# Divisors of the first attention batch through DRAM, weight pieces on SyncE's queue, additions behind both thresholds

## The chip, the cores and the metric

The kernel runs on one core of a Trainium2 chip. The metric is device time in microseconds (us). TensorE is called PE here, its weight loads PEld, VectorE DVE, ScalarE ACT, GpSimd POOL, and SyncE SP. An instruction that starts a transfer sits in the queue of the engine that issues it: POOL's transfers form one queue (q0, software), SP's another (q1, hardware), ACT's a third (q10).

## The reference

A thresholded attention, and then a two-layer network with an exact GELU on its output. All is float32, but the two weight matrices come as float64.

```python
# q, k, v: (8 batches, 8 heads, 576 positions, 64); tau = 0.02
scores = scale * q @ k.T                      # scale = 1/sqrt(64)
thresh = max(scores, -1) - tau
scores = where(scores >= thresh, scores, -1e9)
attn = exp(scores - max(scores))
attn = attn / (sum(attn, -1) + 1e-9)
x = (attn @ v) laid out as (8*576, 512)
h = x @ w_in                                  # w_in (512, 2048), float64
g = 0.5 * h * (1 + erf(h / sqrt(2)))
out = g @ w_out                               # w_out (2048, 512), float64
```

## The kernel before, in words

**Slots.** Two heads make a pair `p`; four pairs (`HP`) make a batch, 32 pairs (`NP`) in all. The 576 positions of a pair are cut into four chunks of 128 and a tail of 64 (`NC` = 4). One turn of the main loop over `n` is a *slot*: one chunk `i` of one pair, with both heads in it (for the tail, i = 4, the two heads' 64 positions share one tile of 128 rows). The first batch (`p < EARLY`, slots 0 to 19) runs in two halves: slots 0 to 7 are chunks 0 and 1 of pairs 0, 1, 2, 3; slots 8 to 19 are chunks 2, 3, 4 of the same pairs. Later batches take a pair at a time. The order of instructions on every engine is that of the program; there is no planner.

**What a slot does.** `scores` puts q·k of one chunk into PSUM (PE, L410, two buffers, one for each head). `softmax_head` takes the negated maximum `nmx` of each head (DVE, L422), makes the threshold `thr` from it (POOL, L423) and the exponentials `p` (ACT, L425). `softmax_tail` (DVE, L442) sets to zero what is below the threshold and sums the rest into a divisor; only then are the score buffers free for the next slot's PE work. One slot later `turn_p_early` turns `p` by PE (L356) and ACT copies the result to `pT` (L363, L372). Two slots after a chunk, `weigh_v` or `weigh_half` multiply by v (L545, L569), ACT copies to `xall`, and `divide_early` divides.

**Divisors of the first batch.** POOL adds 1e-9 to each pair of sums (L445), DVE takes the reciprocal in the next slot (`invert`, L451), and `divide_early` spreads the column of 128 reciprocals over 64 rows by a matmul with an identity (PE, L464; ten instructions per pair), ACT copies this to `inv` (L466), and POOL multiplies `xall` by it (L472). It happens in slots 3, 5, 7 and 9 (chunks 0 and 1 of pairs 0 to 3) and in slots 12, 15, 18 and 21 (the rest).

**Divisors of later batches.** `divisors`: DVE adds 1e-9 to all sums of a pair (L480), takes reciprocals (L481) and transposes the tile in blocks of 32 (L483); SP writes it to DRAM (L486) and reads it back so that each row reaches 64 partitions (L492, L494).

**Weights.** The 32 weight pieces (128 x 512 float64, 512 KB each) are loaded into staging places (parts of `xall` and `turned_p`), and turned into float32 during the first batch. `load_piece` starts one load (L183): pieces 0 and 1 from ACT's queue, all others from POOL's. Four are started ahead of slot 0, four more in slots 0 and 2, and then one whenever a piece has left its place. The conversion of a piece is two ACT operations (L202, L203), two DVE operations on integers (L210, L212) and an integer addition on POOL (L226, `add_low_bits`). `convert` at the end of a slot emits some 1.8 pieces' worth; the additions that are due are emitted in the next slot: one right behind the threshold of each head, and what is left behind the second.

**SP before.** In the first batch SP issues the loads of q, k and v of pairs 1 to 3 and of v of pair 0, and then of pairs 4 and 5 (`load`), whose v loads wait for a POOL memset (L264).

**The network.** From slot 8 on `fill` puts matmuls of the first layer (L637) between the steps of the attention, and later of the second (L652); a matmul is emitted only when its weight pieces are converted in program order. `keep_busy` adds idle matmuls in three slots.

Of the kernel before, what the change touches and what calls it, by code (L numbers as in the profile page):

```python
# [8 lines left out]
FP32 = mybir.dt.float32  # L9
# [3 lines left out]
ALU = mybir.AluOpType  # L13
# [5 lines left out]
def kernel(  # L19
# [138 lines left out]
    loaded = [0]  # L158
    converted = [0]

    def load_piece(eng=nc.gpsimd):
        k = loaded[0]
        if k == len(pieces):
            return
        staged = k % 2 and k < len(pieces) - LATER
        if wide and not staged and not x_free:
            return
        dst, src = pieces[k]
        loaded[0] += 1
        if not wide:  # L170
            nc.sync.dma_start(dst, src)
            converted[0] += 1
            load_piece()
            return
        slot = []
        if staged:

            half, at = divmod(k // 2 % 4, 2)
            raw = pd[half].bitcast(U32)[:, at * 2 * PIECE:(at + 1) * 2 * PIECE]
        else:  # L180
            slot = [x_slot()]
            raw = x_rows(slot[0]).bitcast(U32)
        eng.dma_start(raw, src.bitcast(U32))  # L183
        raws.append((dst, raw, slot))
# [228 lines left out]
    def softmax_head(p, i):  # L413

        s = st[p]
        n = len(s["sc", i])
        nmx = small.tile([P, 2], FP32, tag="nmx", name="nmx")
        thr = s["thr", i] = small.tile([P, 2], FP32, tag="thr", name="thr")
        w = s["p", i] = work.tile([P, 2 * S], FP32, tag="p", name="p")
        for e in range(n):  # L420
            sc = s["sc", i][e][:, :, 0:HALF]
            nc.vector.tensor_reduce(nmx[:, e:e + 1], sc, axis=AXIS.XY, op=ALU.max, negate=True)  # L422
            nc.gpsimd.tensor_scalar(  # L423
                thr[:, e:e + 1], nmx[:, e:e + 1], -1.0, tau_eff, op0=ALU.mult, op1=ALU.subtract)
            nc.scalar.activation(  # L425
                w[:, e * S:(e + 1) * S].rearrange("p (h s) -> p h s", h=2), sc, AF.Exp, bias=nmx[:, e:e + 1], scale=1.0)
            add_low_bits(1)

    def softmax_tail(p, i):

        s = st[p]
        sc, thr, w = s.pop(("sc", i)), s.pop(("thr", i)), s["p", i]
        n = len(sc)
        if p < EARLY:
            pair = small.tile([P, 2], FP32, tag="den", name="den", bufs=2 * SLOTS)
            den = [pair[:, e:e + 1] for e in range(n)]
        else:
            at = [e * NC + i if i < NC else 2 * NC for e in range(n)]
            den = [sums[p % 2][:, x:x + 1] for x in at]
        for e in range(n):  # L440
            row = w[:, e * S:(e + 1) * S].rearrange("p (h s) -> p h s", h=2)
            nc.vector.scalar_tensor_tensor(  # L442
                row, sc[e][:, :, 0:HALF], thr[:, e:e + 1], row, op0=ALU.is_ge, op1=ALU.mult, accum_out=den[e])
        if p < EARLY:
            nc.gpsimd.tensor_scalar(pair[:, 0:n], pair[:, 0:n], 1e-9, None, op0=ALU.add)  # L445
            s["sum", i] = pair[:, 0:n]

    def invert(p, i):

        den = st[p]["sum", i]  # L450
        nc.vector.reciprocal(den, den)  # L451

    def divide_early(p, lo, hi):


        s = st[p]
        b, hp = divmod(p, HP)
        tr = ps.tile([P, 512], FP32, tag="mm", name="tr")
        for i in range(lo // P, -(-hi // P)):
            den = s.pop(("sum", i))  # L460
            to = tr[:, i * P - lo:min((i + 1) * P, hi) - lo]
            for e in range(2):
                one_of, cols = (den[:, e:e + 1], ident) if i < NC else (den, ident[:, e * TAIL:(e + 1) * TAIL])
                nc.tensor.matmul(to[e * D:(e + 1) * D, :], lhsT=one_of.to_broadcast([P, D]), rhs=cols, start=True, stop=True)  # L464
        by = dg.tile([P, S], FP32, tag="inv", name="inv")
        nc.scalar.copy(by[:, 0:hi - lo], tr[:, 0:hi - lo])  # L466
        for n, o, at, size in in_blocks(b, lo, hi):
            x, y = x_blk[n][:, hp, o:o + size], by[:, at - lo:at - lo + size]
            if size == TOK:
                x = x.rearrange("q (p c) -> q c p", c=2)  # L470
                y = y.rearrange("q (c p) -> q c p", c=2)
            nc.gpsimd.tensor_tensor(x, x, y, op=ALU.mult)  # L472

    def divisors(p):

# [10 lines left out]
        flat = rows.rearrange("a k i -> a (k i)")  # L488
        for e in range(2):
            to = t[e * D:(e + 1) * D]  # L490
            src = flat[:, e * P:(e + 1) * P].unsqueeze(0).to_broadcast([D, 4, P])
            eng.dma_start(to[:, 0:MAIN].rearrange("p (a x) -> p a x", x=P), src)  # L492
            src = rows[2 * e:2 * e + 2, 2 * NC, :].unsqueeze(0).to_broadcast([D, 2, Q])
# [597 lines left out]
    for n in range(len(slots) + WEIGH + 1):  # L1091
# [3 lines left out]
        if p < NP:  # L1095
            scores(p, i)
            softmax_head(p, i)
            add_low_bits()
            if last and last[0] < EARLY:
                invert(*last)  # L1100
            if p < HP - 1 and i == 0:
                turn_qk_early(p + 1)
        elif n == len(slots):
# [26 lines left out]
            turn_p_early(*last)  # L1130
        if p < NP:
            softmax_tail(p, i)
        if p < NP and not early:
            turn_p(p, i)
        if p < NP and not early:
# [89 lines left out]
```

## Time and profile before

| | |
|---|---|
| median of 3 runs | 1340.18 us (1338.49 to 1342.54) |
| the profiled execution | 1340.39 us, of which the span is 1338.6 |
| PE busy | 1320.5 us, 99% of the span |
| DVE / ACT / POOL busy | 1043.3 / 604.9 / 656.0 us |
| granted PE clock | 1.00 |
| first batch, slots 0 to 19 | 10 to 136 us |
| chain that ended last | PE 93%, DVE 2%, DMA, ACT, POOL and issue 1% each |

The slots can be found in the trace by the start of their maximum (L422): slot 0 at 10.16 us, 1 at 15.18, 2 at 19.70, 3 at 24.70, 4 at 31.15, 5 at 36.68, 6 at 43.12, 7 at 49.12, 8 at 54.80, 9 at 61.13, 10 at 67.20, 11 at 71.73, 12 at 77.71, 13 at 86.00, 14 at 91.25, 15 at 97.10, 16 at 106.29, 17 at 111.75, 18 at 118.75, 19 at 125.38, 20 at 130.12.

A busy PE is not a PE at its peak: the ends of matmuls are modelled, and a matmul that waits in the pipeline counts as busy. So the chain of waits and the order in time say more here than the share of busy time. The trace holds two records for each float32 matmul instruction.

### The profile page before, as it was taken

How to read it: one execution, taken by the hardware profiler on the slowest of the kernel's cores; microseconds unless marked ns; L12 is line 12 of the kernel's file. 1: busy time of each engine (PE TensorE's matmuls, PEld its weight loads, DVE VectorE, ACT ScalarE, POOL GpSimd, SP SyncE). 2: the span in 40 equal slices, each digit the busy share in tenths (PEclk: the TensorE clock that was granted, in tenths of full speed). 3: DMA queues.
4: the chain of work that ended last, by engine and by line, in shares of the span. 5: the costliest groups of instructions: out<-in, count | busy, mean ns of one | idle time of the engine just before them, and what ended most of it. 6: DMA issues, size and time to landing. Idle time of an engine off the chain costs nothing.

```text
span 1338.6 us, 19954 instructions
## 1 busy us (share of the span) xinstructions
PE 1320.5 (99%) x6354; PEld 893.9 (67%) x6354; DVE 1043.3 (78%) x2005; ACT 604.9 (45%) x1029; POOL 656.0 (49%) x1091
## 2 busy tenths in 40 slices
PE   8899999999999999999999999999999999999998
PEld 6677466466466466457557557568787787877877
DVE  6877778788888888888888888784857698385775
ACT  7877458258357358338438437322211113211120
POOL 5875455555555556545555551245264503635530
PEclk9999999999999999999999999999999999999999
DMA  8652565776786786786787776400000130000003
GB/s 266 190 164 46 121 151 137 166 185 154 173 190 153 176 204 153 176 213 155 164 216 166 162 187 128 108 9 0 1 0 1 38 99 22 1 1 0 1 0 79
DMA packets 209783, 152.41 MB, mean 114 GB/s; under 512 B 113360, under 2 KB 193088, under 8 KB 209680
## 3 DMA queue, kind: packets, MB, share of 16 engines
q1 hardware_dynamic: 187648, 110.43, 36.1%
q0 software_dynamic: 21312, 39.37, 10.7%
q10 hardware_dynamic: 720, 1.34, 0.4%
q8 instruction: 52, 0.85, 0.3%
q14 instruction: 51, 0.42, 0.1%
HBM read 55.97 MB, written 12.52 MB: 51 GB/s over the span
## 4 chain that ended last, share of the span: by engine, by line
PE 93%; DVE 2%; DMA 1%; ACT 1%; POOL 1%; issue 1%; SPq 0%; DVEq 0%; POOLq 0%; ACTq 0%
PE bank L825 34%; PE o_ps L652 17%; PE hT L637 16%; PE sc L410 13%; PE xT L545 12%; DMA q<-in_q_dram 1%; DVE power L212 1%; DMA v<-in_v_dram 1%; POOL w_in L226 1%; DVE nmx L422 0%; PE tr L356 0%; ACT p L425 0%; DVE power L210 0%; ACT pT L363 0%; PE tr L464 0%
## 5 line engine op out<-in xcount | busy, mean ns | idle before, releaser
L425 ACT ACTIVATE p<-sc,nmx 128x576 f32<-128x576 f32 x288 | 201.7, 738 | 275.0 <-DVE nmx L422 274.8
L442 DVE SCALAR_TENSOR_TENSOR p<-sc,thr,p 128x576 f32<-128x576 f32 x288 | 226.4, 816 | 78.1 <-ACT p L425 68.2
L423 POOL TENSOR_SCALAR thr<-nmx,tau_eff 128x1 f32<-128x1 f32 x288 | 84.5, 293 | 359.8 <-DVE nmx L422 350.3
L637 PE MATMUL hT<-xall,w_in 128*128 128x256 f32 x1024 | 242.0, 386 | 0.2 <-POOL xall L472 0.2
L422 DVE TENSOR_REDUCE nmx<-sc 128x1 f32<-128x576 f32 x288 | 205.4, 750 | 43.7 <-PE sc L410 42.4
L652 PE MATMUL o_ps<-w_out,g 128*128 128x512 f32 x512 | 236.8, 603 | 0.0
L637 PEld LDWEIGHTS hT<-xall,w_in 128*128 128x128 f32 x1024 | 189.3, 190 | 50.5 <-issue 23.0
L707 DVE TENSOR_TENSOR c<-c,bank 128x320 f32<-128x320 f32 x304 | 147.0, 487 | 33.8 <-PE bank L825 20.5
L707 DVE TENSOR_TENSOR o<-o,bank 128x256 f32<-128x256 f32 x240 | 99.8, 419 | 93.7 <-PE bank L825 88.7
L652 PEld LDWEIGHTS o_ps<-w_out,g 128*128 128x128 f32 x512 | 93.1, 190 | 109.1 <-issue 106.3
L410 PE MATMUL sc<-kT,qT 64*128 64x288 f32 x960 | 161.3, 429 | 2.6 <-DVE p L442 2.6
L545 PE MATMUL xT<-pT,v 128*64 128x320 f32 (+1 forms) x1240 | 159.6, 409 | 0.7 <-DVE pT L367 0.5
L506 DVE STREAM_TRANSPOSE turned_p<-p 128x1152 f32<-128x1152 f32 x112 | 154.4, 1378 | 3.9
L410 PEld LDWEIGHTS sc<-kT,qT 64*128 64x128 f32 x960 | 91.8, 186 | 77.2 <-issue 62.5
L545 PEld LDWEIGHTS xT<-pT,v 128*64 128x64 f32 x1240 | 86.5, 137 | 71.5 <-issue 10.8
L825 PE MATMUL bank<-w_out,c 128*128 128x256 f32 x480 | 120.2, 381 | 0.5 <-DVE o L707 0.5
L269 POOL DMA_DIRECT2D v<-in_v_dram x208 | 110.9, 536 | 4.1 <-issue 2.2
L825 PEld LDWEIGHTS bank<-w_out,c 128*128 128x128 f32 x480 | 89.9, 190 | 18.8 <-DVE o L707 3.0
L878 ACT ACTIVATE c<-c 128x320 f32<-128x320 f32 (+1 forms) x80 | 46.9, 624 | 114.6 <-DVE c L707 114.5
L707 POOL TENSOR_TENSOR c<-c,g 128x320 f32<-128x320 f32 (+1 forms) x40 | 50.5, 1271 | 67.5 <-DVE c L707 67.5
L825 PE MATMUL bank<-t_out,c 128*128 128x256 f32 x320 | 82.8, 381 | 0.0
L825 PE MATMUL bank<-t_out,g 128*128 128x256 f32 x320 | 82.1, 379 | 0.0
(184 smaller groups left out, 1785.5 us busy)
## 6 DMA issues: line engine op xcount, KB each, us to landing
pT<-turned_p SPq DMA_DIRECT2D x448, 160.0 KB, 3.6
pT<-pd_tail SPq DMA_DIRECT2D x112, 80.0 KB, 2.9
q<-in_q_dram POOLq DMA_DIRECT2D x104, 72.0 KB, 3.6
k<-in_k_dram POOLq DMA_DIRECT2D x104, 72.0 KB, 3.1
inv<-turned SPq DMA_DIRECT2D x54, 128.0 KB, 4.0
v<-in_v_dram POOLq DMA_DIRECT2D x156, 40.0 KB, 3.0
out_dram<-o SPq DMA_DIRECT2D x40, 128.0 KB, 2.3
xall<-in_moe_w_out_dram POOLq DMA_DIRECT2D x9, 512.0 KB, 4.2
```

The source lines that it names most:

```text
L269: eng.dma_start(t[r:P:4, e, 0:n, :], rows[:, r * KR:r * KR + n, :])
L410: nc.tensor.matmul(sc[e][:, h, 0:HALF], lhsT=lhsT, rhs=s["kT"][rows, at:at + HALF], start=True, stop=True)
L422: nc.vector.tensor_reduce(nmx[:, e:e + 1], sc, axis=AXIS.XY, op=ALU.max, negate=True)
L423: nc.gpsimd.tensor_scalar(thr[:, e:e + 1], nmx[:, e:e + 1], -1.0, tau_eff, op0=ALU.mult, op1=ALU.subtract)
L425: nc.scalar.activation(w[:, e * S:(e + 1) * S].rearrange("p (h s) -> p h s", h=2), sc, AF.Exp, bias=nmx[:, e:e + 1], scale=1.0)
L442: nc.vector.scalar_tensor_tensor(row, sc[e][:, :, 0:HALF], thr[:, e:e + 1], row, op0=ALU.is_ge, op1=ALU.mult, accum_out=den[e])
L506: nc.vector.transpose(turned_p[:, :, i // 2, 0:NB, i % 2 * Q:(i % 2 + 1) * Q], w.rearrange("p (e b i) -> p e b i", e=2, i=Q))
L545: nc.tensor.matmul(to, lhsT=s["v"][:, e, c, :], rhs=rhs, start=(c == 0), stop=(c == KR - 1))
L637: nc.tensor.matmul(hT[:, j % 2, :], lhsT=w_in_sb[c][:, j * P:(j + 1) * P], rhs=x_blk[n][:, c, :], start=(c == 0), stop=(c == N_DM - 1))
L652: nc.tensor.matmul(o[:, 0:d_model], lhsT=g[j][:, m * P:(m + 1) * P], rhs=w_out_sb[j], start=(j == 0), stop=(j == N_DF - 1))
L707: eng.tensor_tensor(out, a, b, op=ALU.add)
L825: nc.tensor.matmul(to, lhsT=l, rhs=r, start=start and k == 0, stop=k == len(pairs) - 1, skip_group_check=not start)
```

## The change

Three edits, all of which act in the first batch.

1. The divisors of the first batch go through `divisors` too. It is called at the end of `softmax_tail`'s slot for chunk 1 (for chunks 0 and 1) and for the tail (for the others), with a layout of its own for the two halves; `divide_early` keeps only POOL's multiplication, two slots later as before. L445, L451, L464 and L466 go.
2. `load_piece` issues from SP's queue unless told otherwise. Pieces 0 and 1 stay on ACT's queue, 2 and 3 on POOL's; the other 28 move from POOL to SP, each to its place in SP's program order.
3. The call of `add_low_bits(1)` inside the loop over the heads goes. All additions that are due come behind both thresholds of a slot.

```diff
-    def load_piece(eng=nc.gpsimd):
+    def load_piece(eng=nc.sync):
...
             nc.scalar.activation(
                 w[:, e * S:(e + 1) * S].rearrange("p (h s) -> p h s", h=2), sc, AF.Exp, bias=nmx[:, e:e + 1], scale=1.0)
-            add_low_bits(1)
...
-        if p < EARLY:
-            pair = small.tile([P, 2], FP32, tag="den", name="den", bufs=2 * SLOTS)
-            den = [pair[:, e:e + 1] for e in range(n)]
-        else:
-            at = [e * NC + i if i < NC else 2 * NC for e in range(n)]
-            den = [sums[p % 2][:, x:x + 1] for x in at]
+        at = [e * NC + i if i < NC else 2 * NC for e in range(n)]
+        den = [sums[p % 2][:, x:x + 1] for x in at]
...
-        if p < EARLY:
-            nc.gpsimd.tensor_scalar(pair[:, 0:n], pair[:, 0:n], 1e-9, None, op0=ALU.add)
-            s["sum", i] = pair[:, 0:n]
-
-    def invert(p, i):
-
-        den = st[p]["sum", i]
-        nc.vector.reciprocal(den, den)
-
     def divide_early(p, lo, hi):
-        s = st[p]
         b, hp = divmod(p, HP)
-        tr = ps.tile([P, 512], FP32, tag="mm", name="tr")
-        for i in range(lo // P, -(-hi // P)):
-            den = s.pop(("sum", i))
-            to = tr[:, i * P - lo:min((i + 1) * P, hi) - lo]
-            for e in range(2):
-                one_of, cols = (den[:, e:e + 1], ident) if i < NC else (den, ident[:, e * TAIL:(e + 1) * TAIL])
-                nc.tensor.matmul(to[e * D:(e + 1) * D, :], lhsT=one_of.to_broadcast([P, D]), rhs=cols, start=True, stop=True)
-        by = dg.tile([P, S], FP32, tag="inv", name="inv")
-        nc.scalar.copy(by[:, 0:hi - lo], tr[:, 0:hi - lo])
+        by = st[p].pop("inv")
         for n, o, at, size in in_blocks(b, lo, hi):
             x, y = x_blk[n][:, hp, o:o + size], by[:, at - lo:at - lo + size]
             if size == TOK:
-                x = x.rearrange("q (p c) -> q c p", c=2)
-                y = y.rearrange("q (c p) -> q c p", c=2)
+                x = x.rearrange("q (a i c) -> q a c i", i=Q, c=2)
+                y = y.rearrange("q (a c i) -> q a c i", i=Q, c=2)
             nc.gpsimd.tensor_tensor(x, x, y, op=ALU.mult)
 
-    def divisors(p):
+    def divisors(p, chunk=None):
...
         for e in range(2):
             to = t[e * D:(e + 1) * D]
+            if chunk is not None:
+                src = flat[:, (e * NC + chunk) * Q:(e * NC + chunk + 2) * Q]
+                eng.dma_start(to[:, 0:TOK].rearrange("p (a x) -> p a x", x=2 * Q),
+                              src.unsqueeze(0).to_broadcast([D, 4, 2 * Q]))
+                if chunk:
+                    src = rows[2 * e:2 * e + 2, 2 * NC, :].unsqueeze(0).to_broadcast([D, 2, Q])
+                    eng.dma_start(to[:, TOK:TOK + TAIL].rearrange("p (a x) -> p a x", x=Q), src)
+                continue
...
             add_low_bits()
-            if last and last[0] < EARLY:
-                invert(*last)
...
             softmax_tail(p, i)
+        if early and i in (1, NC):
+            divisors(p, 0 if i == 1 else 2)
```

## The prediction

> **What bounds the kernel now.** I read the busy table by stretches first, because the page's own slices are 33 us wide and the change touches only the first batch (slots 0 to 19, 10 to 136 us). Columns: busy us (count) of PE, PE's weight loads, DVE, ACT, POOL, then clock, DMA share, GB/s.
>
> ```profile
> 10.00:26.00 16.00, 14.39 (x136) 9.75 (x135) 12.70 (x27) 14.52 (x32) 7.89 (x16) 1.00 0.94 295
> 26.00:42.00 16.00, 14.98 (x145) 10.75 (x143) 13.38 (x29) 15.43 (x35) 12.63 (x20) 1.00 1.02 253
> 42.00:72.00 30.00, 26.00 (x212) 19.90 (x209) 26.49 (x53) 25.04 (x52) 24.10 (x35) 1.00 0.56 166
> 72.00:136.00 64.00, 60.58 (x368) 45.38 (x368) 49.57 (x99) 49.06 (x99) 41.63 (x66) 1.00 0.37 101
> 136.00:160.00 24.00, 24.00 (x94) 11.65 (x93) 17.10 (x31) 10.63 (x19) 12.75 (x26) 1.00 0.48 104
> ```
>
> From 136 us on PE is never idle, and its queue keeps its order, so whatever the first batch gains or loses is carried to the end nearly whole. Inside the batch the limit changes: to 42 us ACT (15.43 of 16) with the DMA engines full, then DVE and POOL, from 72 us mostly PE. The chain of waits confirms it; two extracts, start, length, what:
>
> ```profile
> 53.07 0.92 POOL xall L472
> 54.08 0.83 POOL den L445
> 54.97 0.62 POOL turned_p L183
> 55.62 0.54 POOL xall L183
> 56.19 0.33 POOL thr L423
> ...
> 76.70 2.84 PE xT L545 x20
> 79.54 0.55 PE tr L464 x12
> 80.09 3.22 PE hT L637 x14
> ```
>
> In slot 7 and 8 the chain runs through POOL work that the change removes (L445, L183); in slot 12 through the L464 matmuls that it removes. The third view is the order in time of DVE and POOL:
>
> ```profile
> 57.73 0.28 POOL L423 TENSOR_SCALAR thr<-nmx,tau_eff 128x1 f32<-128x1 f32 x1
> 57.98 1.27 POOL L226 TENSOR_TENSOR w_in<-power,w_in 128x512 uint32<-128x512 uint32 x1
> 58.05 0.82 DVE L442 SCALAR_TENSOR_TENSOR p<-sc,thr,p 128x576 f32<-128x576 f32 x1 [0.67 <-POOL thr L423]
> 58.79 1.02 DVE L212 SCALAR_TENSOR_TENSOR power<-turned_p,power 128x512 uint32<-128x512 uint32 x1
> ```
>
> L442 waited 0.67 us for a threshold queued behind an addition. But L212, median 693 ns, took 1020: it ended 0.56 us after the addition L226 did (59.81 against 59.25), while L442, beside the same addition, took its usual 0.82. So an addition holds up the DVE conversions, not the softmax.
>
> **What the Trainium skill says.** "SBUF — State Buffer", section Who interferes with whom: VectorE and GpSimd share one pair of ports as an exclusive lock, taken by a VectorE operation with two SBUF inputs or in a two-port mode; the other one blocks fully. The lines above agree (L212 has two SBUF inputs; L442 reads scores from PSUM). "DMA: Bandwidth & Descriptors", section Queues, rings and completion order: an engine takes turns between queue rows packet by packet, and within a row consumes descriptors in ring order. Before, weight pieces lie on POOL's row and small loads on SyncE's; no run here yet shows both in one row. Same page, SWDGE vs HWDGE: SyncE's transfers need no descriptors written by GpSimd; in the trace each L183 costs POOL about 0.6 us.
>
> **The change, part by part.** All against the profiled execution, 1340.39 us (span 1338.6); the median shown is 1340.18, 0.2 lower.
>
> 1. L464 leaves PE: 10 instructions per pair, 80 trace records. In the later half (slots 12, 15, 18, 21) PE is the chain and they cost 0.55, 0.55, 0.55 and 0.71 us: **-2.4**. In slots 3, 5, 7, 9 the next limit is ACT, DVE or POOL; the 0.37 us copy L466 leaves ACT too, which counts in slots 3 and 5, but there part 4 takes its place: 0 (low end -1).
>
> 2. POOL loses 20 L445 (0.23 to 0.89 us) and 24 L183 (about 0.6 each). Mostly this is no limit: L423 usually waits for nmx, not for POOL. In slot 8 POOL is late: nmx was ready at 55.47, slot 7's L423 followed it by 0.26, here it started at 56.19: **-0.46**. DVE loses 20 reciprocals (0.15 spacing, 3.0 in all) and gets 8 times L480, L481, L483 (spacing in later batches 160.1 to about 160.8, 0.7; 5.6 in all). The reciprocals lay ahead of L442, which waited for ACT or POOL anyway. The new three stand behind L442, ahead of the conversions, partly while an addition holds the port: between 0 and +2.6, taken as **+0.5**.
>
> 3. Additions behind both thresholds. In slot 6 thr of head 0 came at 44.07, the first addition at 44.35, the second threshold at 45.60, the second addition ended at 47.12. Now both thresholds go first (the second can start 0.26 after nmx ends at 44.45, so the first addition starts near 45.0) and the two additions end near 47.5. The second L442 no longer waits (0.34 in most slots), but the conversions behind it need the port and get it 0.37 later. Five slots (4, 6, 7, 9, 11) show L210 or L212 stretched by an addition and followed at once by the next nmx: 5 x 0.37 = **+1.9**. Bounds: 0, if DVE gets in between two additions (in slot 16 L210 at 108.66 did); below nothing, -1.7, if L442's wait of 0.34 is what counts in five slots; above, +3 for eight slots.
>
> 4. Divisors through DRAM, on the same queue as the pieces. Each early pair now needs twice: L480 to L483, a write to DRAM (landing 1.9 us in later batches), SyncE waiting for it, two reads (four in the second half; 0.6 issue each, 3.4 to 5.7 to land), then the multiplication on POOL two slots later. Queued behind that multiplication are both thresholds of the next slot, for which L442 waits, then PE's scores. Between L442's end two slots earlier and L472 before there are 11.1 us (28.9 to 40.07, slots 3 to 5), 12.7 (40.4 to 53.07), 12.0 (69.65 to 81.68); the trip takes 7 to 10: nothing, as long as SyncE is free. At the start it isn't.
>    - First pair: SyncE reaches its first pieces at about 23.3 (v of pair 2 started at 23.83), then v, and issues the write near 27. Ahead of it in the row: two pieces and v, 1.34 MB, at 264 GB/s 5.1 us from about 25. The write lands near 31, reads are issued to 31.8 and land near 35. The multiplication (0.74) stood at 28.55, slot 4's threshold at 32.09; now 36.0: 3.9 late. ACT, which bound slots 4 and 5, absorbs the 0.67 that L442 waited for it in slot 5: **+3.2** (0 to 5).
>    - Second pair: four pieces and v of pair 3, with the reads 2.5 MB, enter from 32.2 on: row empty near 42, write landed 43, reads landed 47. Slot 6's threshold is due at 44.07 + 3.2, so they are needed by 46.6: **+0.4** (0 to 6).
>    - Later pairs follow three to five pieces each, a 5.5 to 9 us backlog, within the margin. Pieces were issued from 14.63 on by POOL and now start at 23.3, but the first of these is read by ACT at 29.85 and the next at 31.0, 36.9, 41.3: about the time they land, cover thin. That the early loads get the row to themselves from 14.6 to 23 is worth nothing: the list of waits has no engine waiting for a load from 14 to 31 us, and where the chain names one (v, landed 24.75) PE was on scores to 24.67. Also moved behind: the loads of pair 4 (q, k), which SyncE ran ahead with at 29 to 42 and now issues in slot 13 (about 90 to 105), still before ACT scales them near 115: nothing.
>
> Sum: -2.4 - 0.46 + 0.5 + 1.9 + 3.2 + 0.4 = **+3.1**, so 1343.5 as profiled, 1343.3 as a median.
>
> **Rivals.**
> - *SyncE's row saturates* (slower). Each write waits behind pieces, and the next pieces wait until SyncE has seen it land, so the row runs dry twice per two slots. For: 26 to 42 us show the DMA engines full at 253 GB/s. Against: the loads of pair 4, in short runs, leave that stretch. At 220 GB/s the first stall is 4 us, the second about 5.5, and the third pair misses its slot too by some 2: 11.5 in place of 3.6, so 1351. It decides when the reads for pair 1 land later than about 47 us.
> - *The stalls don't come* (faster). The write isn't held up by the row (16 KB among pieces of 512 KB), or ACT's slack absorbs it; DVE gets in between additions, and L442's 0.34 us waits go. Then -2.4 - 0.8 (L464 and L466 in slots 3, 5) - 0.46 - 1.7 = -5.4: 1335. For: the chain names POOL and L464; against: the margin in slot 3 is under 10 us, with full DMA engines.
> - *Nothing to measure*: gains (3 us) and costs cancel, 1340. If the additions keep their order in effect (thresholds were ready anyway), only parts 1 and 4 count, -2.4 + 3.6.
>
> **How the numbers follow.** A measurement of this kernel can tell about 0.3%, 4 us, from no change. Forecast 0.45, its own range 1340 to 1347, of which 0.20 lies above 1344.2; saturated row 0.30; cancelled 0.13; no stalls 0.12. So slower 0.50, same 0.25 + 0.13 = 0.38, faster 0.12. The range leaves out the outer ends of both rivals: 1335.5 to 1354.
>
> **What would show it.** POOL's multiplication in slot 3 preceded by an idle time of some 6 us released by the read of inv, and thr of slot 4 near 36 us; the same once more in slot 5, and none from slot 7 on. L442 without waits on thr, but L210 and L212 longer. No L464 between xT and hT, and the start of that xT in slot 12 later than 76.7 us by 4 to 6. After 136 us the same PE sequence, shifted by 2 to 4 us. The forecast is wrong if slot 4's threshold comes before 33 us, if waits on inv recur in slots 9 to 18, or if the batch ends (xT at 135.58) more than 8 us late or at all early.

## The result, and the profile after

The changed kernel takes 1348.59 us in the median of 6 runs (1348.17 to 1349.57), beside 1339.24 for the kernel before: a ratio of 1.0068, with a 95% interval from 1.0056 to 1.0080. It is slower by about 9 us. The prediction said 1343.3, in a range from 1335.5 to 1354. The profiled execution took 1348.58 us, its span 1346.8, 8.2 more than the span before.

In the kernel after, some lines have moved: L442 is now L437, the multiplication L472 is L449, the three instructions of `divisors` L480, L481, L483 are L459, L460, L462, the write L486 is L465, the reads are L472 and L476 (in experiments that add lines they are one or more lines off). xT is L532 and L556, hT L624.

The busy table by stretches (columns as in the prediction):

```profile
26.00:42.00 16.00, 11.43 (x88) 7.90 (x86) 10.46 (x22) 10.97 (x24) 4.78 (x6) 0.86 0.70 232
42.00:72.00 30.00, 25.92 (x197) 19.69 (x194) 26.65 (x51) 23.95 (x48) 15.41 (x22) 0.85 0.51 162
72.00:136.00 64.00, 59.91 (x319) 43.65 (x318) 51.61 (x96) 45.74 (x93) 31.79 (x42) 0.97 0.51 149
136.00:160.00 24.00, 22.88 (x105) 12.29 (x103) 18.75 (x37) 13.89 (x24) 11.29 (x24) 1.00 0.34 71
```

From 26 to 42 us PE, DVE and ACT have lost 22 to 29% of their busy time (ACT 10.97 us, 15.43 before), and TensorE's granted clock is 0.86, where before it was 1.00. The chain of waits (start, length, what) names the cause of the first stop:

```profile
27.03 3.62 DMA turned<-turned
30.67 0.61 SPq L472
...
31.33 4.40 DMA inv<-turned
...
35.90 0.73 POOL xall L449
36.63 0.28 POOL thr L423
...
37.82 3.02 PE sc L410 x8
40.85 4.02 PE xT L532 x20
```

Write, read, multiplication, and only then the threshold of slot 4, for which the scores wait. The threshold came at 36.63 us, 32.09 before: 4.54 late. From there to the next maximum it took 4.52 us, 4.59 before, so slot 4 gave nothing back; in both kernels DVE's conversions run up to that maximum and end the slot. The order in time of POOL in the kernel before had the first two multiplications, and the threshold of slot 4 between them, here:

```profile
28.55 0.74 POOL L472 TENSOR_TENSOR xall<-xall,inv 128x256 f32<-128x256 f32 x1 [0.64 <-ACT inv L466]
...
32.09 0.31 POOL L423 TENSOR_SCALAR thr<-nmx,tau_eff 128x1 f32<-128x1 f32 x1 [0.36 <-DVE nmx L422]
...
40.07 0.74 POOL L472 TENSOR_TENSOR xall<-xall,inv 128x256 f32<-128x256 f32 x1 [0.63 <-ACT inv L466]
```

In the kernel after it has the four multiplications of chunks 0 and 1, with the idle time ahead of each:

```profile
35.90 0.73 POOL L449 TENSOR_TENSOR xall<-xall,inv 128x256 f32<-128x256 f32 x1 [8.84 <-DMA inv<-turned]
...
49.60 0.73 POOL L449 TENSOR_TENSOR xall<-xall,inv 128x256 f32<-128x256 f32 x1 [5.43 <-DMA inv<-turned]
...
59.56 0.75 POOL L449 TENSOR_TENSOR xall<-xall,inv 128x256 f32<-128x256 f32 x1
...
71.91 1.20 POOL L449 TENSOR_TENSOR xall<-xall,inv 128x256 f32<-128x256 f32 x1
```

Two waits, in slots 3 and 5, and none afterwards. What was not foreseen is in the same windows cut to 1 us, TensorE alone (busy, clock, DMA share, GB/s):

```profile
36.00:37.00 1.00, 0.00 (x0) 1.00 0.96 336
37.00:38.00 1.00, 0.18 (x1) 0.73 0.99 406
38.00:39.00 1.00, 1.00 (x4) 0.50 1.03 407
...
43.00:44.00 1.00, 1.00 (x8) 0.50 0.00 0
44.00:45.00 1.00, 1.00 (x10) 0.85 0.05 13
```

From 37.46 us, 0.36 before the stop ended, TensorE ran at half its clock for 6.8 us: the scores took 3.02 us (1.24 in experiment 6, where the clock stays full), xT 4.02 (2.38). The Trainium skill, "TensorE: Matmul & The Clock Gate", section What's actually happening, describes this: the clock is halved after an idle window of about 3.4 us, and given back after a busy one. The stop, a gap of 3.37 us, agrees; the way back less so, since TensorE was at work again from 37.82 us on and had its full clock only at 44.29.

The best tool for what follows is a table by slot, worked out from the starts of L422: length of a slot less its length before, in us, each from one profiled execution. "To 21" is slot 0 to the start of slot 21, "rest" from there to the end of the span, both in full.

| | 0-3 | 4 | 5 | 6 | 7 | 8 | 9 | 10 | 11 | 12 | 13 | 15 | 16 | 18 | 19 | 20 | to 21 | rest |
|---|---|---|---|---|---|---|---|---|---|---|---|---|---|---|---|---|---|---|
| before | | | | | | | | | | | | | | | | | 126.13 | 1202.3 |
| after | +.14 | +4.80 | +.87 | +.87 | +.56 | -.21 | +.27 | +.82 | +.27 | -1.24 | +.74 | -.61 | +.76 | +.69 | +.44 | -.40 | 134.51 | 1202.6 |
| 1 pieces on POOL | +.30 | +7.23 | +.31 | +.26 | +.55 | -.20 | +.27 | +.64 | +.28 | -1.15 | +.76 | -.61 | +.79 | +.68 | +.45 | -.40 | 135.93 | 1203.7 |
| 3 additions only | +1.81 | +.26 | -.23 | +.26 | +.28 | -.03 | +.26 | +.01 | +.28 | -.69 | -.01 | -.41 | +.01 | -.27 | .00 | -.39 | 127.24 | 1202.5 |
| 5 second half only | -.26 | .00 | +.02 | -.01 | +.02 | .00 | -.01 | +.64 | -.02 | -.56 | +.77 | -.38 | +.80 | -.58 | +.44 | -.01 | 126.80 | 1203.5 |
| 6 idle matmuls | +.31 | +2.89 | -.52 | +1.86 | +.97 | -.19 | +.26 | +.81 | +.27 | -1.25 | +.75 | -.60 | +.76 | -.96 | +.44 | -.40 | 131.16 | 1204.2 |
| 9 two later | +.62 | +.68 | +.51 | +.68 | +.40 | +.52 | -.28 | +2.67 | +.28 | -1.26 | +.77 | -.59 | +.76 | +.69 | +.44 | -.39 | 132.26 | 1204.9 |
| 11 two later, POOL | +.10 | +.26 | +.64 | +.68 | +.55 | -.19 | +.27 | +.64 | +.28 | -1.15 | +.77 | -.61 | +.79 | -.95 | +.44 | -.40 | 127.87 | 1206.4 |

Left out are slots 14 (-.39 at most) and 17 (within .01). Of the 8.4 us of the changed kernel, 7.1 come in slots 4 to 7, 1.2 in slots 8 to 11, and what slots 12 to 20 win and lose cancels. Slots 0 to 3 and the rest differ by 1 to 4 us between executions, without an edit that accounts for it; slots 12 to 20 repeat within 0.1 us between kernels with the same edits there, where the clock is full, so they show each edit by itself.

### The profile page after: what moved, and what is told of

Read it like the earlier page. It is cut to its first block, busy times and chain, and to the rows that moved or that the text cites. A ratio compares the mean times of both kernels' runs of the same rounds, so it can differ in the third digit from the quotient of the medians.

```text
span 1346.8 us, 19820 instructions
## 1 busy us (share of the span) xinstructions
PE 1322.2 (98%) x6274; PEld 893.4 (66%) x6274; DVE 1050.0 (78%) x2009; ACT 602.9 (45%) x1021; POOL 629.3 (47%) x1043
## 3 DMA queue, kind: packets, MB, share of 16 engines
q10 hardware_dynamic: 720, 1.34, 0.4%
## 4 chain that ended last, share of the span: by engine, by line
PE 91%; DVE 3%; DMA 2%; ACT 2%; issue 1%; SPq 0%; POOL 0%; DVEq 0%; ACTq 0%; POOLq 0%
PE bank L812 34%; PE o_ps L639 17%; PE hT L624 16%; PE sc L410 13%; PE xT L532 11%; ACT p L425 1%; DVE power L212 1%; DVE p L437 1%; DVE nmx L422 1%; DMA turned<-turned 1%; DMA q<-in_q_dram 1%; DVE power L210 0%; DMA x<-xall 0%; DMA xall<-in_moe_w_out_dram 0%; DMA inv<-turned 0%
## 5 line engine op out<-in xcount | busy, mean ns | idle before, releaser
L437 DVE SCALAR_TENSOR_TENSOR p<-sc,thr,p 128x576 f32<-128x576 f32 x288 | 225.4, 815 | 79.8 <-ACT p L425 72.5
L624 PE MATMUL hT<-xall,w_in 128*128 128x256 f32 x1024 | 242.0, 386 | 0.4 <-POOL xall L449 0.4
L422 DVE TENSOR_REDUCE nmx<-sc 128x1 f32<-128x576 f32 x288 | 205.2, 749 | 43.2 <-PE sc L410 42.1
L624 PEld LDWEIGHTS hT<-xall,w_in 128*128 128x128 f32 x1024 | 189.3, 190 | 52.0 <-issue 24.5
L532 PE MATMUL xT<-pT,v 128*64 128x320 f32 (+1 forms) x1240 | 161.9, 415 | 0.6 <-DVE pT L367 0.5
L532 PEld LDWEIGHTS xT<-pT,v 128*64 128x64 f32 x1240 | 87.5, 139 | 73.5 <-issue 14.2
```

The lines of the kernel that those rows point to most:

```text
L437: nc.vector.scalar_tensor_tensor(row, sc[e][:, :, 0:HALF], thr[:, e:e + 1], row, op0=ALU.is_ge, op1=ALU.mult, accum_out=den[e])
L532: nc.tensor.matmul(to, lhsT=s["v"][:, e, c, :], rhs=rhs, start=(c == 0), stop=(c == KR - 1))
L624: nc.tensor.matmul(hT[:, j % 2, :], lhsT=w_in_sb[c][:, j * P:(j + 1) * P], rhs=x_blk[n][:, c, :], start=(c == 0), stop=(c == N_DM - 1))
```

## The experiments

**1. The changed kernel, its pieces back on POOL's queue.**

```diff
-    def load_piece(eng=nc.sync):
+    def load_piece(eng=nc.gpsimd):
```

> The changed kernel with the 28 pieces back on POOL's queue (divisors through DRAM and additions behind both thresholds stay). Row theory: the two stalls come from the write of the sums standing behind pieces in SyncE's row. SyncE still issues v of pair 2 first, so the write goes out near 26 us, lands near 28, the reads land near 32: POOL's multiplication in slot 3 waits 4 to 5 us in place of 8.8, slot 4's threshold comes near 33 (36.6 in the changed kernel), no wait in slot 5; 1340 to 1344 us. Rival, full engines: the trip is long because the 16 DMA engines are full from 26 to 42 us whatever the row; then the waits stay near 9 and 5 us and the time at 1347 to 1349.

Measured: 1351.55 us, 1.0081 (1.0066 to 1.0096). SP's queue and POOL's multiplication, from the order in time:

```profile
25.89 0.53 SPq L465 DMA_DIRECT2D turned<-turned  x1
32.86 1.27 SPq L472 DMA_DIRECT2D inv<-turned  x2
36.56 0.53 SPq L465 DMA_DIRECT2D turned<-turned  x1
38.30 1.27 SPq L472 DMA_DIRECT2D inv<-turned  x2
```

```profile
37.13 0.74 POOL L449 TENSOR_TENSOR xall<-xall,inv 128x256 f32<-128x256 f32 x1 [10.15 <-DMA v<-in_v_dram]
...
47.26 0.74 POOL L449 TENSOR_TENSOR xall<-xall,inv 128x256 f32<-128x256 f32 x1 [0.67 <-ACT xall L542]
```

With no piece in SP's row, the first write took 7.0 us to land instead of 3.6, and the first stop is longer. So the first stop needs no piece in the write's row. But that row was not empty. Loads of v stood ahead of the write in it, and the last of these landed at 32.67 us, 0.17 before the write; in the changed kernel it was 30.47, and the write 30.65. Meanwhile the pieces filled the DMA engines from POOL's row, until the last one landed at 32.19. The order of landings fits a write that waits for v, while v shares the engines with the pieces, whichever row they are in. A write with nothing ahead of it in its row was not tried at this time. The second write landed in 1.7 us instead of 4.8, and the second stop is gone. That one comes from the pieces, which in the changed kernel lie just ahead of the write (the last landed at 42.91, the write at 43.07); but it is not shown that their row is the reason, since POOL's pieces now also start later, behind its multiplication (DMA shares of 0.33 and 0.00 from 37 to 39 us).

**2. and 3. The pieces alone, and the additions alone,** each put into the kernel before.

```diff
# 2
-    def load_piece(eng=nc.gpsimd):
+    def load_piece(eng=nc.sync):
# 3
-            add_low_bits(1)
```

> The kernel before with one edit: the 28 pieces on SyncE's queue. Row theory: without a round trip in that row nothing waits for SyncE, and POOL is no limit, so within 1 us of the kernel before (1338.5 to 1340.5). Rival, late pieces: pieces start at 23.7 us in place of 14.6 and ACT waits for them (2.0 us in slot 4 of the changed kernel); then 1341 to 1343.

> The kernel before with one edit: all additions behind both thresholds. Port theory: the conversions on DVE get the shared port 0.37 us later in about five slots: plus 1.9 us, 1341 (1339.5 to 1342.5), with L210 or L212 stretched to 1.4 to 1.7 us right behind the second L442. Rival, waits gone: L442 no longer waits for a threshold behind an addition (0.34 us in many slots): minus 1.7 us, 1337.5.

Measured: 1341.63 us, 1.0009 (0.9998 to 1.0020), and 1339.52, 0.9990 (0.9979 to 1.0001): neither can be told from nothing. With the pieces alone, slot 8 is 0.49 us shorter, as the prediction had it for a POOL that is on time, but slot 9 is 0.32 longer. The table says more on the additions: they lengthen slots 4, 6, 7, 9 and 11 by 0.26 to 0.28 us each, 1.34 in all, and shorten slots 12, 15, 18 and 20 by 1.76. In slot 6 DVE shows both (order in time; L441 is L442 of the kernel before):

```profile
46.55 0.82 DVE L441 SCALAR_TENSOR_TENSOR p<-sc,thr,p 128x576 f32<-128x576 f32 x1
...
47.30 0.81 DVE L441 SCALAR_TENSOR_TENSOR p<-sc,thr,p 128x576 f32<-128x576 f32 x1
...
48.04 1.44 DVE L210 TENSOR_SCALAR power<-power 128x512 uint32<-128x512 uint32 x1
```

The second of the two no longer waits 0.34 us for its threshold, but the conversion behind it takes 1.44 us in place of 0.75, since the two additions now follow each other. Where conversions end the slot that is a loss; where TensorE's scores wait for the second one, a gain.

**4. The divisors alone:** the changed kernel, with the pieces and the additions as before.

```diff
-    def load_piece(eng=nc.sync):
+    def load_piece(eng=nc.gpsimd):
...
+            add_low_bits(1)
```

> The kernel before with one edit: the divisors of the first batch through DRAM. Row theory: as with the additions moved too, one short stall in slot 3 (multiplication waits to about 32 us), none in slot 5; minus 2.4 us for the matmuls gone in slots 12, 15, 18 and 21, plus about 1 for the stall and 0.5 for the three new DVE operations: 1338 to 1342. Full engines: plus 6 or more, 1345. Clock theory: with the L464 matmuls gone PE idles more in slots 3 to 9, and its granted clock falls below 1.00 in the stretch from 26 to 72 us even without long stalls; row theory alone says nothing on the clock.

Measured: 1351.7 us, 1.0088 (1.0073 to 1.0104). The whole loss is in this edit. The other two, together, make it smaller by some 3 us in the medians; the intervals of this run and of the changed kernel overlap, so that much isn't settled.

**5. The divisors of chunks 2 to 4 alone,** chunks 0 and 1 as before: in the kernel before, `divisors(p, 2)` is called behind the tail of a pair, and L464 and L466 stay for the first half only.

```diff
+        if early and i == NC:
+            divisors(p, 2)
```

> The kernel before with only chunks 2, 3 and 4 of the first batch divided through DRAM (slots 12, 15, 18, 21); chunks 0 and 1 keep the matmuls, pieces stay on POOL's queue, additions between the thresholds. No trip at the start, so no stall. Sum of the prediction: minus 2.4 us of PE, plus 0.3 for DVE: 1338. Rival, DVE: L480, L481 and L483 stand behind an addition that holds the port in slots 13, 16 and 19 and cost 0.7 each there, also in slot 10: plus 2.1 to 2.8, so within 0.5 us of the kernel before.

Measured: 1345.04 us, 1.0039 (1.0024 to 1.0053); its profiled execution, 1342.44, was the quickest of the six. The table separates two terms. In slots 12, 15 and 18 (and 21, by 0.55), without L464, it is quicker by 0.56, 0.38 and 0.58. In slots 10, 13, 16 and 19, where the three DVE instructions stand, it is slower by 0.64, 0.77, 0.80 and 0.44: 2.65 in all. No slot waits for inv. The changed kernel repeats these slots. They explain under 1 us of this run's loss; for the rest see below.

**6. The changed kernel with idle matmuls in slots 4 and 7,** to keep TensorE's clock up.

```diff
-    BUSY = {6: 2, 8: 2, BATCH: 4}
+    BUSY = {4: 6, 6: 2, 7: 3, 8: 2, BATCH: 4}
```

> The changed kernel with idle matmuls ahead of the scores of slots 5 and 8 (BUSY of slot 4: 6, of slot 7: 3), where PE waits and its granted clock falls to 0.50 afterwards. The matmuls lie in PE's wait, the stalls of POOL stay as they are. Clock theory: the scores and xT of slot 5 take 1.2 and 2.6 us again (3.0 and 4.1 in the changed kernel), those of slot 8 likewise; minus 2 to 3 us of the 9, 1346. Rival: DVE, not PE, ends these slots, so the slow PE is covered: within 1 us of the changed kernel, 1348 to 1349.

Measured: 1348.30 us, 1.0069 (1.0055 to 1.0082), no gain. Its windows, all engines:

```profile
26.00:42.00 16.00, 14.16 (x134) 10.69 (x130) 11.66 (x24) 12.92 (x27) 5.93 (x10) 1.00 0.70 231
42.00:72.00 30.00, 23.10 (x201) 17.42 (x197) 27.19 (x51) 23.36 (x47) 15.83 (x21) 1.00 0.53 173
```

The clock stayed at 1.00. Slot 5 is 1.39 us shorter than in the changed kernel, but slots 6 and 7 are 1.40 longer, since POOL then waits for inv all the same: slots 5 to 7 together lose 2.31 us, 2.30 in the changed kernel. Slot 4 is 1.91 shorter, but not by the clock. In this execution it began 1.04 us later (31.86) and its threshold came 1.06 earlier (35.57), so the wait in it was shorter; from the threshold to the next maximum it took 4.71 us, no less than the 4.52 of the changed kernel, since DVE ends this slot. The idle matmuls, which ran to 39.07 us, even held up the scores. Another 1.65 us come from slot 18, and 1.6 are lost again right after the batch, where the clock is 0.93 from 136 to 160 us. So this half clock is a consequence of the first stop, and what it costs runs beside a wait that lasts anyway.

**7. The changed kernel, with all four trips and multiplications of chunks 0 and 1 one slot later.**

```diff
-        if early and i in (1, NC):
-            divisors(p, 0 if i == 1 else 2)
+        if last and last[0] < EARLY and last[1] == 1:
+            divisors(last[0], 0)
+        if early and i == NC:
+            divisors(p, 2)
...
-            divide_early(*args)
+            if args[1] == 0:
+                later.append(args)      # emitted in the next slot, behind its thresholds
+            else:
+                divide_early(*args)
```

> The changed kernel with the trip for chunks 0 and 1 and its multiplication both one slot later (SyncE's write at the end of slot 2, 4, 6, 8; POOL's multiplication in slot 4, 6, 8, 10). Stall theory: the trip is as long as before, but SyncE is still loading when the first sums are ready, so the first pair gains a slot: the multiplication in slot 4 waits under 2 us, no threshold is late, PE's clock stays at 1.00; minus 5 to 7 us, 1342 to 1344. Rival: the loss lies in the slots (port, DVE, pieces late), not in the two waits: 1347 or more.

Measured: 1351.3 us, 1.0081 (1.0067 to 1.0095). Slots 4 to 7 are only 1.2 us longer than before. But slot 10 took 9.26 us more: the last multiplication, at 73.42, is what the first hT matmuls read, and TensorE, which keeps its order, waited 6.53 us for it. The wait moved, and cost as much.

**8. As experiment 1, with v of pairs 2 and 3 loaded behind the first two trips in SP's queue.**

```diff
+        if p < 2 and i == 1:
+            load_v_early(p + 2)
```

> The kernel with divisors through DRAM, additions behind both thresholds and pieces on POOL's queue (1351.6), with the v loads of pairs 2 and 3 behind the first two trips in SyncE's queue. Order theory: the first write stood behind these loads in SyncE's queue; it goes out at 23.2 us in place of 25.9, and the multiplication in slot 3 waits to about 33 to 34 (37.1): minus 3 to 5 us, 1347 to 1349. Full engines: the write lands when the pieces of POOL's row are through, about 32 us, whenever it went out: wait unchanged, 1350 to 1352.

Measured: 1350.85 us, 1.0082 (1.0068 to 1.0095). SP's queue:

```profile
24.17 0.57 SPq L465 DMA_DIRECT2D turned<-turned  x1
32.47 1.27 SPq L472 DMA_DIRECT2D inv<-turned  x2
```

The write was issued earliest of all, with no piece and less v ahead of it in its row, and yet took 8.3 us. The last v ahead of it landed at 31.16 us, the last piece on POOL's queue at 32.23, the write at 32.41. In the trace of the DMA packets its own (128 of 128 bytes) run from 28.06 to 31.89 us, beside the last ones of v (to 30.62) and of the pieces (to 31.72). The share of the DMA engines is 0.77 to 1.11 from 23 to 30 us and falls to 0.11 at 31. So pieces on another row hold a write up too. The row counts all the same: in the changed kernel the first three writes landed at 30.65, 43.07 and 54.12, each 0.16 to 0.18 us after the last load ahead of it in SP's row (v at 30.47, pieces at 42.91 and 53.96). So in these kernels a write waited for what stood ahead of it in its row, and that went more slowly while another row filled the engines.

**9. The changed kernel, with the multiplications of pairs 0 and 1 alone one slot later;** their trips stay where they are.

```diff
-            divide_early(*args)
+            if args[0] < 2 and args[1] == 0:
+                later.append(args)      # emitted in the next slot, behind its thresholds
+            else:
+                divide_early(*args)
```

> The changed kernel, but POOL's multiplications for chunks 0 and 1 of pairs 0 and 1 are emitted one slot later (in slots 4 and 6, behind both thresholds of those slots), while the trips through DRAM stay where they are; the divisors of pair 1 get a tile of their own for it. Nothing else moves, pairs 2 and 3 included. Theory 'the loss is the two waits of POOL ahead of thresholds': slots 4 to 7, which took 27.2 us in the changed kernel and 23.7 before (starts of slot 3 to slot 8: 37.6 and 30.1), come back to within 1 us of before, TensorE's clock stays at 1.00, and the time is 1342 (1340.5 to 1343.5): of the loss of 9.4 only what DVE's three instructions per pair cost in slots 10, 13, 16, 19 is left, less the gain of TensorE. Rival 'what hurts is the DMA engines' load, which delays the weight pieces and v whatever POOL does': the waits on inv go, but ACT waits for pieces in slots 4 to 7 instead, and the time is 1346 or more. Rival 'the wait moves on, as it did to the first layer's matmuls when all four pairs were shifted': the reads for pair 1 land after 48 us, slot 7's thresholds are late by 1 to 2 us, and the time is 1344.

Measured: 1347.84 us, 1.0047 (1.0034 to 1.0061). The two stops are gone, slots 4 to 7 take 4.8 us less than in the changed kernel (where they took 30.75 us, not the 27.2 of the expectation), and TensorE's clock is 1.00 from 26 to 120 us. Yet most of it is not gained. POOL:

```profile
35.81 1.02 POOL L449 TENSOR_TENSOR xall<-xall,inv 128x256 f32<-128x256 f32 x1 [0.46 <-DMA inv<-turned]
...
48.47 0.93 POOL L449 TENSOR_TENSOR xall<-xall,inv 128x256 f32<-128x256 f32 x1
...
58.26 0.74 POOL L449 TENSOR_TENSOR xall<-xall,inv 128x256 f32<-128x256 f32 x1 [3.06 <-DMA inv<-turned]
...
70.68 0.74 POOL L449 TENSOR_TENSOR xall<-xall,inv 128x256 f32<-128x256 f32 x1 [2.55 <-DMA inv<-turned]
```

Now pairs 2 and 3 wait, in slots 7 and 9, and hT in slot 10 waits 2.51 us for the last of them. In the changed kernel these two multiplications came at 59.56 and 71.91 without a wait only because everything ahead was already 6 to 7 us late. The trip for pair 2 takes from 46.67 (write issued) to 58.1 (reads landed), that for pair 3 from 56.88 to 70.5: 12 and 14 us. Their writes landed 0.17 and 0.16 us after the piece ahead of them in SP's row. The "wait moves on" was expected for pair 1; it came at pairs 2 and 3.

**10. As 9, and the divisors of chunks 2 to 4 emitted behind the slot's conversions.**

```diff
-        if early and i in (1, NC):
-            divisors(p, 0 if i == 1 else 2)
+        if early and i == 1:
+            divisors(p, 0)
...
         convert(0 if n == 0 else 1200 if n < 3 else 1900 if n < BATCH - 1 else 1e9)
+        if early and i == NC:
+            divisors(p, 2)
```

> As the run with the multiplications of pairs 0 and 1 one slot later, and besides the divisors of chunks 2 to 4 (DVE's addition, reciprocal and transpose, and the trip that hangs on them) are emitted behind the slot's conversions instead of ahead of them, in slots 10, 13, 16 and 19. Theory 'the three DVE instructions stand behind a weight addition that holds the port and delay DVE there': slots 10, 13, 16 and 19 are shorter by 0.4 to 0.8 us each than in the run without this, 2 us in all, and the time is 1340; the reads still land two slots later in good time. Rival 'these slots are longer because the conversions and the next maximum wait for something else (the port, PSUM)': no difference of over 1 us in their sum, and the time is as without it. Rival 'the trip comes too late now': POOL's multiplication in slots 12, 15, 18, 21 waits for inv, and the time is longer by 1 to 3 us.

Measured: 1345.64 us, 1.0037 (1.0023 to 1.0051), not to be told from experiment 9. Slots 13, 16 and 19 are 0.54, 0.61 and 0.35 longer than before, against 0.77, 0.76 and 0.44; slot 10, where hT waits for POOL, is 3.16 longer, against 2.67. Over the four slots nothing is gained. DVE in slot 13, first of the changed kernel, then of this one (order in time):

```profile
95.58 1.04 DVE L459 TENSOR_SCALAR sums<-sums 128x9 f32<-128x9 f32 x1
96.65 0.21 DVE L460 RECIPROCAL sums<-sums 128x9 f32<-128x9 f32 x1
96.90 0.21 DVE L462 STREAM_TRANSPOSE turned<-sums 128x32 f32<-128x32 f32 x1
97.04 0.65 DVE L212 SCALAR_TENSOR_TENSOR power<-xall,power 128x512 uint32<-128x512 uint32 x1
```

```profile
93.51 1.45 DVE L212 SCALAR_TENSOR_TENSOR power<-xall,power 128x512 uint32<-128x512 uint32 x1
...
95.94 0.17 DVE L459 TENSOR_SCALAR sums<-sums 128x9 f32<-128x9 f32 x1
96.14 0.22 DVE L460 RECIPROCAL sums<-sums 128x9 f32<-128x9 f32 x1
96.39 0.21 DVE L462 STREAM_TRANSPOSE turned<-sums 128x32 f32<-128x32 f32 x1
```

Whichever comes first behind the softmax waits for the additions on POOL: L459 took 1.04 us in place of 0.17 and ended at 96.62, POOL's additions at 96.34; in the other order L212 took 1.45 in place of 0.69 and ended at 94.96, the additions at 94.40. The Trainium skill, "SBUF — State Buffer", section Who interferes with whom, has both kinds of instruction among those that can need the shared ports. The wait is paid once in either order, and the three instructions cost their own 0.6 us besides, since in these slots the next maximum follows DVE's conversions at once.

**11. As 9, with the pieces on POOL's queue** (the diff is that of 1).

> As the run with the multiplications of pairs 0 and 1 one slot later, but with the weight pieces on POOL's queue again, so that nothing but the small loads shares SyncE's row with the divisors. With the pieces on SyncE's row the reads of inv for pairs 2 and 3 landed at 58.2 and 70.7 us in every kernel that did not stall earlier. Theory 'the row itself sets that pace: each write stands behind three or four pieces, each read behind the write': now the trips of pairs 1 to 3 take under 6 us from the write's issue to the reads' landing (12 to 14 before), POOL has no wait on inv in slots 6, 7 and 9 and the first layer's matmuls none on POOL in slot 10; slots 4 to 10 together take within 1.5 us of the 36.4 us that they took in the kernel before (starts of slot 4 to slot 11: 31.15 to 71.73 is 40.6), and the time is 1342 to 1343.5: what is left is DVE's 2.6 us in slots 10, 13, 16 and 19 and perhaps 1 us in slot 5, less 2.4 of TensorE. Rival 'the DMA engines' load sets it, whichever row': the first trip takes 12 us and ends at 37, that is behind slot 4's thresholds and costs little, but pairs 2 and 3 still wait 2 to 3 us each and the time stays at 1346 to 1348. Rival 'POOL now issues its pieces behind a multiplication that waits': ACT waits for pieces in slots 5 and 6 by 2 us and more, and the time is 1344 to 1346.

Measured: 1345.95 us, 1.0037 (1.0023 to 1.0051). SP's queue, pairs 1 to 3:

```profile
37.21 0.53 SPq L465 DMA_DIRECT2D turned<-turned  x1
38.97 1.27 SPq L473 DMA_DIRECT2D inv<-turned  x2
...
41.91 0.34 SPq L465 DMA_DIRECT2D turned<-turned  x1
46.27 1.24 SPq L473 DMA_DIRECT2D inv<-turned  x2
...
55.39 0.33 SPq L465 DMA_DIRECT2D turned<-turned  x1
56.87 1.24 SPq L473 DMA_DIRECT2D inv<-turned  x2
```

The writes take 1.8, 4.4 and 1.5 us where in the changed kernel those of pairs 1 to 3 took 4.8, 8.2 and 5.8. POOL waits for inv no more in slots 6, 7 and 9, and hT for POOL only 0.37 us. Slots 4 to 10 are 2.85 us longer than before, where within 1.5 was expected (before, they took 40.6 us, not 36.4): the table shows the additions (0.27 a slot in 4, 6, 7 and 9), DVE's 0.64 in slot 10, 0.64 in slot 5, where the first multiplication still came late (37.92), and 0.7 beyond the additions in slots 6 and 7. Slot 0 to slot 21 is only 1.7 us longer than before. This kernel is faster than the changed one, by intervals that do not meet, but still slower than the kernel before. It shows that the long trips of pairs 2 and 3 came from the pieces on SP's queue; how much of that is the row, and how much the time at which they start, it does not tell, since on POOL's queue they also start at other times. The write of pair 2 is a hint: it had no open load ahead of it in its row and still took 4.3 us, beside a piece on POOL's queue that landed at 46.04, 0.18 before it.

**12. The kernel before, with the additions behind both thresholds from slot 12 on only.** Of all that was found this pointed to a version quicker than both.

```diff
-            add_low_bits(1)
+            if (p, i) < (1, 3) or (p < EARLY and i < 2):
+                add_low_bits(1)
```

> The kernel before, with the additions behind both thresholds from slot 12 on only; in slots 0 to 11 one stands behind the threshold of each head, as before. Read off slot by slot, the additions alone made slots 4, 6, 7, 9 and 11 longer by 0.26 to 0.28 us each (1.34 in all: DVE's conversions get the port later) and slots 12, 15, 18 and 20 shorter by 0.69, 0.41, 0.27 and 0.39 (1.76 in all: there the second L442 no longer waits 0.34 us for its threshold, and TensorE's scores hang on it). Theory 'the two are separate and each belongs to its slot': slots 4 to 11 are within 0.1 us each of the kernel before, slots 12, 15, 18 and 20 are shorter by 1.8 in all, and the time is 1338.5 beside 1340.2, a gain of 0.13% that the comparison may just not tell from none. Rival 'the gain in slot 12 is work that was put off in slots 4 to 11, and comes only with their loss': slot 12 is as before, 1 us at most is gained, and the time is 1339.5 to 1340.

Measured: 1338.9 us, 0.9994 (0.9985 to 1.0002): no gain that can be told from none. Slots 4 to 11 are as before within 0.01, slots 15, 18 and 20 shorter by 0.43, 0.27 and 0.38 as expected, but slot 12 by 0.00: its 0.69 was work put off in earlier slots, as the rival had it.

## Why the prediction was right, and where it was wrong

**The sign, and the mechanism of the first stop, were right.** The reads landed at 35.73 us (35 predicted), the threshold of slot 4 came at 36.63 (36.0). Of the signs named: POOL idle ahead of the multiplication in slot 3 (8.84 us; some 6 was said), again in slot 5 (5.43), none from slot 7 on; xT of slot 12 late by 7.2 us (4 to 6 was said); the last xT of the batch at 143.49, late by 7.9, just inside the 8 that was named as a sign of being wrong; after 136 us the shift stays (the rest of the span is 1202.6 us, 1202.3 before). The size was not right: the loss is three times the forecast's, and 1348.6 lies outside the forecast's own range of 1340 to 1347. Only the wider range, which takes in the rivals, holds it, and that much is luck.

**Term by term,** in us, from the slots:

| term | predicted | measured |
|---|---|---|
| L464 leaves PE (slots 12, 15, 18, 21) | -2.4 | -2.07 (experiment 5) |
| POOL on time in slot 8 | -0.46 | -0.2 (experiment 2: -0.49, and +0.32 in slot 9) |
| three DVE instructions | +0.5 (0 to 2.6) | +2.65 |
| additions | +1.9 (-1.7 to +3) | +1.34 in the five slots named, -1.76 in slots 12, 15, 18, 20 |
| first stop (slot 4) | +3.2 | +4.5 (4.80 less 0.26 of the additions) |
| second stop (slots 5 to 7) | +0.4 (0 to 6) | at most +1.8 (2.30 less 0.54) |
| half clock in slot 18 | none | about +1.65 (+0.69, against -0.96 with full clock) |

- *First stop.* The path and its first half were right: the write stood behind two pieces and v in SP's row and landed at 30.65 us, 0.18 after the last v, for "near 31". The size was not: the threshold came 4.54 us late instead of 3.9, and the 0.67 us that ACT was to absorb in slot 5 did not show, since slot 5 ran in part at half clock (0.87 us longer than before; 0.52 shorter with the clock held, experiment 6). The working also took the pieces in the row for necessary. They are not: on POOL's queue (1 and 8) they slow down the v loads ahead of the write, which lands no sooner.
- *Second stop.* The write landed at 43.1 as predicted (43), but the reads at 49.5 instead of 47; the three pieces issued right behind them, at 44.57 to 45.65, ran beside them. In 1, with the pieces elsewhere and later, this stop is gone, though slots 5 to 7 still lose 1.1 us; so the stop as such is worth less than the whole 1.8.
- *"Later pairs ... within the margin."* This step failed behind a sign that looked right. There were no waits on inv from slot 7 on, but because the slots were late, not because the trips were short: 9 and 11 show trips of 12 and 14 us with the pieces in the row, and waits of 2.5 to 3 us once the first two stops are removed. That is the rival of the saturated row, whose third pair misses its slot, and its time, 1351, is nearer to the result than the forecast.
- *DVE.* The term was mis-sized: it lay just above the upper end of its own bounds. The reciprocals that leave gave nothing back, as argued; the three that come are paid in full, wherever they stand (10).
- *Additions.* The five slots are the five that the prediction named, at 0.27 each rather than 0.37. The gain in PE's slots was overlooked, though its lower bound had the mechanism.

**What stays open.** The profiles of experiments 5 and 11 show 0.7 and 1.7 us more than before up to slot 21, their medians 5 to 6 us more. Part of it goes with the clock: over 134 timed executions (the kernel before and experiments 1 to 11), each against the mean of its own kernel, 0.001 less in mean granted clock goes with 0.74 us more; the kernel before averages 0.998, experiments 5 and 11 0.996 and 0.997, and the profiled execution of 5 had 1.000. In the profile of 11 the clock is 0.50 from 594.4 to 601.2 us, and slots 108 to 111, which lie there, lose 4.3 us; the clock can explain 3.4 of them. Reduced to full clock by that rate, 5 is still some 3 us above the kernel before. Why kernels with the divisors through DRAM are granted less, and where that remainder lies, was not found.

## What to carry to other kernels

An engine that keeps its order turns one late operand into a wait for everything behind it, so before a short on-chip step is replaced by a trip through memory, ask what stands behind its consumer, what stands ahead of it in its queue, and how full the DMA engines are at that time: an emptier queue alone did not help here. A wait that is absent from the profile may be absent because an earlier one hides it: remove the first, and see what is late next. Compare by slots or stages of the same work: there, edits of 0.3 us can be told apart that no median shows.

## What the hardware showed that was not expected

- TensorE's clock went to 0.50 three times in the first batch of the changed kernel, for 6.8 us (from 37.46), 6.8 (57.94) and 3.4 (122.80). The section of the skill named above gives an idle window of about 3.4 us as the cause, and a busy one as the way back. The lengths agree, being once and twice that. The causes do so less: in the 3.41 us ahead of the three stretches TensorE was busy for 0.40, 1.36 and 1.87 us, and its gaps were 3.37, 2.05 and 1.54 us. In the first 3.41 us of the two long stretches it was busy for 3.05 us and throughout, and the clock did not come back yet. Nor is a short gap enough: in experiment 9 one of 2.5 us before 71.47 was followed by no such stretch, and of ten profiles with a gap of 1.4 to 1.6 us in slot 17 only four show one right behind it. What decides was not found.
- One 16 KB write to DRAM took from 1.5 us (experiment 11, pair 3) to 8.3 us (experiment 8, first pair) from its issue to the issue of the reads that wait for it; the prediction had reckoned with 1.9 where nothing is in the way. All four of chunks 0 and 1 in the changed kernel landed 0.16 to 0.18 us after the last load ahead of them in SP's row. With no open load ahead in the row, but pieces running on POOL's, it took 3.6 us (experiment 8, pair 2) and 4.3 (experiment 11, pair 2).
